# Where the products with v, the tail's score maxima, two copies and one v halving stand in a fused attention and two-MLP kernel

## The chip, the core and the metric

One core of a Trainium2 chip runs the kernel. The metric is device time in microseconds (us), the median of the runs. The engines are TensorE (PE, with its weight loads shown apart as PEld), VectorE (DVE), ScalarE (ACT), GpSimd (POOL) and SyncE (SP), whose queue issues every DMA here.

## The reference, cut to what matters

```python
# q, k, v: [4, 8, 576, 64], f: [4, 8, 576], all float32
scores = q @ k^T / 8 + (cum[:, :, :, None] - cum[:, :, None, :])   # cum = cumsum(log f); causal
attn = softmax(scores)                                             # rows of 576, masked above the diagonal
x  = (attn @ v) -> [2304, 512]                                     # heads side by side
x1 = (s * relu(x @ w_in)**2 + b) @ w_out                           # d_ff 2048
out = leaky(x1 @ w2_in, 0.01) @ w2_out                             # d_ff 2048
```

## The kernel before

Tokens are cut into nine units: for each of the 4 batches the first 256 positions ("first" units), for each batch the next 320 ("rest" units, of which the last 64 positions are the tail), and one unit that gathers the four tails' results. The first MLP works unit by unit, in 16 steps each. A step does h (12 products, L941), then g on ACT and DVE (Relu, Square, copy to the high half on ACT, the low half by a subtraction on DVE), then o (12 products, L990) with the g of two steps earlier. Each float32 operand is split in a high and a low half, hence three products for one. The first two units run together ("joint"), and the second MLP follows after the last unit.

The attention of later units is laid between the first MLP's steps. A **pair** of heads of a rest unit takes four steps; there are 16 such pairs, one after another:

- step 0: scores of 128 queries against 512 keys for both heads (tile `ps_s`); per head a score maximum on DVE (L334, it writes tile `tt`), the exponent on ACT (L356), a high half in f16 on ACT (`p_high`, L410) and a low half on DVE (`p_low`, L415), which a DMA then transposes into `p_t` (L423). Of the second head the halves are written only in the next step ("carry").
- step 1: the same with 384 keys.
- step 2: the tail, 64 queries of both heads against 576 keys, in the middle of the step, after h.
- step 3: no scores; the next pair's v is scaled and halved (L241 to L260) and transposed into `v_st`.

The products of p with v (`av_mm`, L467) come three steps after their scores: of the 512-key tiles in step 3, of the 384-key tiles in the next pair's step 0, of the tail in its step 1. `av_copy` (ACT, L493) and `av_add` (DVE, L497) then bring the two halves of the product together in `x_raw` or `x_l`.

All of that is written inside `in_order()`: on each engine instructions run exactly in the order of the code, so an engine whose next instruction waits holds back everything behind it. `ps_s` is a single buffer: new scores wait until the maxima of the former ones are taken. The pool `tt` has 4 buffers, `p_hl` 3.

At the end of the joint units `mlp1_end` reads four sums out of PSUM through `x1o` tiles (pool `tt`) in turn on ACT (L1018) and DVE (L1020), each followed by a DMA to DRAM. This stands in the first step of the third unit, while two `tt` buffers still hold exponents that wait for `diags` (DVE, L381 to L715) and the products that turn them (L725).

Of the kernel before, what the change touches and what calls it, by code (L numbers as in the profile page):

```python
# [8 lines left out]
F32 = mybir.dt.float32  # L9
# [8 lines left out]
P = 128  # L18
UN = 256
# [20 lines left out]
def attention_moe_moe_kernel(  # L40
# [274 lines left out]
    def st_score(i):  # L315
        mm_score(i)
        score_max(i)
        score_exp(i)
# [166 lines left out]
    def av_copy(i):  # L485
        jb, n, ts, last = tiles[i]
        u, h, j, half = jobs[jb]
        if last and not half and h % 2 == 0:
            x_raw[j // 2] = xp.tile([P, UN], F32, tag="x_raw", name="x_raw", bufs=1)
        if half:  # L490
            x_l[j // 2] = xp.tile([P, NL], F32, tag="x_l", name="x_l", bufs=1)
        for o, own, oth in av_parts(i):
            nc.scalar.copy(o, oth)  # L493
# [302 lines left out]
    plan = {}  # L796

    def at_step(n):
        return plan.setdefault(n, {k: [] for k in ("v", "s", "av", "x", "turn", "first", "load")})

    t_of = {}
    for i, (jb, *_) in enumerate(tiles):
# [2 lines left out]
    for p in range(H, NP):  # L805
        ids = t_of[p]
        at_step(nxt)["s"] = ids[:2]
        if len(ids) == 2:
            at_step(nxt + 1)["turn"] = at_step(nxt + 2)["first"] = ids
            nxt += 2  # L810
            if len(t_of[p + 1]) > 2:
                at_step(nxt)["load"].append(p + 1)
                at_step(nxt + 1)["v"].append((p + 1, 0))
                nxt += 2
                at_step(nxt)["v"].append((p + 1, 1))
        else:
            for k in range(3):
                at_step(nxt + k)["s"] = ids[2 * k : 2 * k + 2]
                at_step(nxt + 3 + k)["av"] += ids[2 * k : 2 * k + 2]
            at_step(nxt + 6)["x"].append(ids[-1])  # L820
            if p + 1 < NP:
                at_step(nxt + 3)["v"] += [(p + 1, 0), (p + 1, 1)]
            nxt += 4
# [17 lines left out]
    def attend(n):  # L841
        e = at_step(n)
        first = e["s"] and len(t_of[jobs[tiles[e["s"][0]][0]][2] // 2]) == 2
        tail = e["s"] and jobs[tiles[e["s"][0]][0]][3]
        if ended:
            mlp1_end(*ended.pop())
        dg.update({k: diags(k) for k in e["turn"]})
        if e["first"]:
            k = e["first"][-1]
            first_x(3, jobs[tiles[k][0]][1] // 2, pair_av(3, k))  # L850
        for i in e["av"]:
            av_mm(i)
        if e["s"] and not tail:
            mm_score(e["s"][0])
        for i in carry:
            p_high(i)
            p_low(i)
        carry.clear()
        for i in e["av"]:
            av_copy(i)  # L860
        if tail:
            assert not e["av"]
            return
        for i in e["s"]:
            score_max(i)
        for i in e["s"]:
            score_exp(i)
        if len(e["v"]) > 1:
            v_part(*e["v"].pop(0))
        for k, i in enumerate(e["s"]):  # L870
            if not first:
                p_scale(i)
            if k == 0:
                for a in e["av"]:
                    av_add(a)
        if not e["s"]:
            for a in e["av"]:
                av_add(a)
        if not first:
            for i in e["s"][:1]:  # L880
                p_high(i)
                p_low(i)
            carry.extend(e["s"][1:])

    dg = {}

    def attend_mid(n):
        e = at_step(n)
        turn_pair(e["turn"])
        for i in e["s"]:  # L890
            if jobs[tiles[i][0]][3]:
                st_score(i)
                p_scale(i)
                p_high(i)
                p_low(i)
# [51 lines left out]
                )  # L947
        return ps

    def mlp1_g(u, i, ps):  # L950

        n = UN + 2 * (u == UB)
        if joint[0]:
            r = r_all.rearrange("p u n -> p (u n)")
            g = gp.tile([P, 2, 2 * UN], F32R, tag="g", name="g", bufs=2)
            nc.scalar.activation(r, ps, AF.Relu)  # L956
            nc.scalar.activation(r, r, AF.Square)
            nc.scalar.copy(g[:, 0], r)
            rest.append(lambda: nc.vector.tensor_tensor(out=g[:, 1], in0=r, in1=g[:, 0].bitcast(F32), op=ALU.subtract))
            return g  # L960
        if u != UB:
            if i % 2 == 0:
                kept["g"] = gp.tile([P, 2, 2, UN], F32R, tag="g", name="g", bufs=2)
            g = kept["g"][:, i % 2]
        else:
            g = gp.tile([P, 2, UN + 2], F32R, tag="g", name="g", bufs=2)
        if u == UB:
            nc.gpsimd.memset(g[:, 0, UN:].bitcast(F32), 1.0)
            nc.gpsimd.memset(g[:, 1, UN:].bitcast(F32), 0.0)
        nc.scalar.activation(ps, ps, AF.Relu)  # L970
        nc.scalar.activation(ps, ps, AF.Square)
        nc.scalar.copy(g[:, 0, :UN], ps)  # L972
        nc.vector.tensor_tensor(out=g[:, 1, :UN], in0=ps, in1=g[:, 0, :UN].bitcast(F32), op=ALU.subtract)  # L973
        return g[:, :, :n]

# [22 lines left out]
    def mlp1_end(u, po):  # L998
        if 1 < u < UB:
            b, u0 = units[u][:2]  # L1000
            for k, po in enumerate(po):
                if k == 0:
                    o = wt_tile().bitcast(F32).rearrange("p (k n) -> p k n", k=2)
                    nc.scalar.mul(o, po, sb[:, 0:1])
                else:
                    o = r_all
                    nc.vector.tensor_scalar(o, po, sb[:, 0:1], None, ALU.mult)  # L1007
                last = nc.sync.dma_start(
                    out=x1d[2 * k * P : 2 * (k + 1) * P, b * S + u0 : b * S + u0 + UN].rearrange("(k p) t -> p k t", p=P),
                    in_=o,  # L1010
                )
            return last
        for d in (2, 1, 0, 3) if u < 2 else range(ND):
            x1 = x1d[d * P : (d + 1) * P, :]
            if u < 2:
                o = ap.tile([P, S], F32, tag="tt", name="x1o", bufs=4)[:, : 2 * UN]
                if d % 2 == 0:
                    nc.scalar.mul(o, po[d], sb[:, 0:1])  # L1018
                else:
                    nc.vector.tensor_scalar(o, po[d], sb[:, 0:1], None, ALU.mult)  # L1020
                last = nc.sync.dma_start(
                    out=x1.rearrange("p (b s) -> p b s", b=B)[:, :2, :UN], in_=o.rearrange("p (b s) -> p b s", b=2)
                )
                continue
            if d == 0:
                o2 = wt_tile().bitcast(F32).rearrange("p (k n) -> p k n", k=2)
            o = (r_all if d < 2 else o2)[:, d % 2]
            if u == UB:
                nc.vector.tensor_scalar(bw1[:, d : d + 1], po[d][:, UN : UN + 1], sb[:, 1:2], None, ALU.mult)
            if d % 2 == 0:  # L1030
                nc.scalar.mul(o, po[d][:, :UN], sb[:, 0:1])
            else:
                nc.vector.tensor_scalar(o, po[d][:, :UN], sb[:, 0:1], None, ALU.mult)
            if u < NU - 1:
                b, u0 = units[u][:2]
                last = nc.sync.dma_start(out=x1[:, b * S + u0 : b * S + u0 + UN], in_=o)
            else:
                last = nc.sync.dma_start(
                    out=x1.rearrange("p (b s) -> p b s", b=B)[:, :, S - NL :],
                    in_=o.rearrange("p (b s) -> p b s", b=B),  # L1040
                )
        return last
# [134 lines left out]
        pending.append((1, i, g))  # L1177
        high(w1, c_of, i)

    def first_mlp(u, i, mid=lambda: None):  # L1180
        ps = mlp1_h(u, i)
        g = mlp1_g(u, i, ps)
        mid()
        while pending and (len(pending) > 1 or pending[0][0] == 1 or u == UB):
            mlp1_back(u)
        pending.append((u, i, g))

    last = None
    for u in range(1, NU):
# [12 lines left out]
        for i in range(NF):  # L1202
# [10 lines left out]
            if u < NU - 2:  # L1213
                n = (u - 2) * NF + i
                with in_order():
                    if n == 0:
                        rest.pop()()
                        for k in range(ND):
                            first_x(2, k, x_held[k])
                    attend(n)  # L1220
                    if n == 1:
                        attend_mid(n)
                        first_mlp(u, i)
                    else:
                        first_mlp(u, i, lambda: attend_mid(n))
                    attend_end(n)
                continue
            with in_order():
# [98 lines left out]
```

## Time and profile before

| | us |
|---|---|
| median of 3 runs | 1025.35 (1024.13 to 1030.38) |
| the profiled execution, its own time | 1027.19 |
| its span, first to last instruction | 1025.3 |
| PE busy in the span | 977.6 (95%) |
| DVE busy | 526.1 (51%) |
| ACT busy | 502.2 (49%) |

The engines' shares are means over stages: the short pairs of the first units end near 205 us, the 16 long pairs run from 210 to about 511, and from there on PE has hardly any pause. A wait is put down to the instruction that released it; whether that instruction sets the pace has to be followed further back.

### The profile page before, as it was taken

To read this page: it belongs to the slowest core of one execution; us is meant where nothing else is said; L and a number is where in the kernel's file an instruction comes from. 1 tells how busy PE (TensorE), PEld (TensorE's weight loads), DVE (VectorE), ACT (ScalarE), POOL (GpSimd) and SP (SyncE) were. 2 spreads that over 40 slices of the span, in tenths; PEclk is the share of its full clock that TensorE was granted. 3 is DMA by queue.
4 is the path that set the end of the run, shared out by engine and by line. 5 is a ranking of instruction groups with operands and counts; after the bars stand their busy time and mean duration, and the time that the engine had idled before them with its cause. 6 is when DMAs were issued, how large, how long until landed. Compare 5 with 4: busy or idle time off the path is not lost.

```text
span 1025.3 us, 17139 instructions
## 1 busy us (share of the span) xinstructions
PE 977.6 (95%) x6464; PEld 835.4 (81%) x6464; DVE 526.1 (51%) x1383; ACT 502.2 (49%) x1196; POOL 27.7 (3%) x100
## 2 busy tenths in 40 slices
PE   5899998989999999999999999999999999999998
PEld 3667776878888888888899998888888888888897
DVE  5888763357677677677612379886111211211111
ACT  4777664556667666666643466543212222221232
POOL 1000000000000000000000000000000000000000
PEclk9999999999999999999999999999999999999999
DMA  8844022359989989889410497002100100100010
GB/s 289 302 131 162 21 82 66 93 112 177 199 174 182 188 169 205 182 159 195 92 43 1 148 376 258 1 1 73 52 1 1 61 1 1 42 1 1 1 42 21
DMA packets 157074, 110.32 MB, mean 108 GB/s; under 512 B 110592, under 2 KB 135168, under 8 KB 156992
## 3 DMA queue, kind: packets, MB, share of 16 engines
q1 hardware_dynamic: 156992, 109.23, 42.7%
q8 instruction: 51, 0.84, 0.3%
q14 instruction: 31, 0.25, 0.1%
HBM read 74.00 MB, written 10.04 MB: 82 GB/s over the span
## 4 chain that ended last, share of the span: by engine, by line
PE 53%; DMA 1%; DVE 0%; issue 0%; POOL 0%; ACT 0%; POOLq 0%
PE ps_o L1090 20%; PE ps_h L1074 19%; PE ps_o L990 6%; PE ps_h L941 6%; DMA p_t<-p_hl 0%; PE ps_v L467 0%; DMA p_t<-p_hl_t 0%; PE ps_s L300 0%; PE ps_s L287 0%; DVE p_hl_t L415 0%; POOL v_hl L254 0%; ACT p_hl_t L410 0%; DVE r_all L1007 0%; DVE o L1102 0%; DVE vs L241 0%
## 5 line engine op out<-in xcount | busy, mean ns | idle before, releaser
L941 PE MATMUL ps_h<-x_all,w 128*128 128x256 f32 (+1 forms) x1536 | 232.6, 300 | 1.2 <-ACT r_all L956 0.7
L990 PE MATMUL ps_o<-g,w 128*128 128x256 f32 (+2 forms) x1536 | 227.8, 297 | 2.7 <-DVE r_all L1007 2.7
L1090 PE MATMUL ps_o<-w,g 128*128 128x512 f32 x864 | 215.0, 395 | 0.0
L990 PEld LDWEIGHTS ps_o<-g,w 128*128 128x128 f32 x1536 | 203.2, 189 | 14.2 <-DVE r_all L1007 3.5
L1074 PE MATMUL ps_h<-x,w 128*128 128x512 f32 (+1 forms) x960 | 213.5, 370 | 0.0
L941 PEld LDWEIGHTS ps_h<-x_all,w 128*128 128x128 f32 x1536 | 202.7, 190 | 11.4 <-issue 1.2
L1074 PEld LDWEIGHTS ps_h<-x,w 128*128 128x128 f32 x960 | 169.1, 188 | 34.4
L1090 PEld LDWEIGHTS ps_o<-w,g 128*128 128x128 f32 x864 | 161.0, 188 | 37.5
L1082 DVE TENSOR_TENSOR g<-ps_h,g 128x512 fp32r<-128x512 f32 (+1 forms) x80 | 50.9, 637 | 248.7 <-ACT g L1081 248.4
L1080 ACT ACTIVATE ps_h<-ps_h 128x512 f32<-128x512 f32 (+1 forms) x80 | 43.1, 539 | 263.2 <-PE ps_h L1074 263.2
L356 ACT ACTIVATE tt<-tt,sm 128x512 f32<-128x512 f32 (+4 forms) x128 | 76.1, 597 | 91.6 <-DVE sm L334 91.6
L973 DVE TENSOR_TENSOR g<-ps_h,g 128x256 fp32r<-128x256 f32 x112 | 47.3, 422 | 98.3 <-ACT g L972 97.6
L970 ACT ACTIVATE ps_h<-ps_h 128x256 f32<-128x256 f32 x112 | 40.9, 366 | 52.9 <-PE ps_h L941 52.9
L334 DVE CUSTOM_DVE_ANT_0 tt<-ps_s,cumk 128x512 f32<-128x512 f32 (+4 forms) x128 | 58.8, 497 | 4.4 <-PE av L734 2.0
L467 PE MATMUL ps_v<-p_t,v_st 128*128 128x128 f16 (+1 forms) x768 | 44.3, 208 | 15.3 <-DMA p_t<-p_hl_t 8.7
L467 PEld LDWEIGHTS <-v_st 128*128 128x128 f16 x768 | 36.7, 98 | 19.6 <-issue 17.3
L415 DVE SCALAR_TENSOR_TENSOR p_hl<-tt,sm,p_hl 128x512 f16<-128x512 f32 (+1 forms) x64 | 43.9, 685 | 8.0 <-ACT p_hl L410 6.3
L1081 ACT CAST g<-ps_h 128x512 fp32r<-128x512 f32 (+1 forms) x80 | 43.5, 544 | 6.5 <-PE ps_o L1090 4.1
L300 PE MATMUL ps_s<-qk_p 64*128 64x512 f32 (+3 forms) x224 | 44.4, 492 | 1.5 <-DVE sm L334 1.3
L114 DVE SCALAR_TENSOR_TENSOR wt<-w_raw,wt 128x512 int32<-128x512 int32 x64 | 44.3, 692 | 2.0
L972 ACT CAST g<-ps_h 128x256 fp32r<-128x256 f32 x112 | 41.7, 372 | 4.3
L109 ACT ACTIVATE wt<-w_raw 128x512 f32<-128x512 f32 x64 | 41.3, 673 | 4.6 <-DMA w_raw<-in_moe_w_in 3.8
(113 smaller groups left out, 785.4 us busy)
## 6 DMA issues: line engine op xcount, KB each, us to landing
w_raw<-in_moe_w_in SPq DMA_DIRECT2D x32, 512.0 KB, 8.3
w_raw<-in_moe_w_out SPq DMA_DIRECT2D x32, 512.0 KB, 9.1
cumk<-cumd SPq DMA_DIRECT2D x32, 256.0 KB, 4.0
qk_p<-in_qk SPq DMA_DIRECT2D x16, 480.0 KB, 4.6
cumk<-cumd SPq DMA_DIRECT2D x32, 144.0 KB, 3.3
v_raw<-in_v SPq DMA_DIRECT2D x16, 288.0 KB, 3.3
out<-o SPq DMA_DIRECT2D x18, 256.0 KB, 2.1
x2r<-x1d SPq DMA_DIRECT2D x4, 1024.0 KB, 5.5
```

The costliest lines, as they stand in the source:

```text
L114: nc.vector.scalar_tensor_tensor(x, top, -0x80000000, x, ALU.bitwise_and, ALU.bitwise_or)
L300: nc.tensor.matmul(ps[:, e, at[r] : at[r + 1]], qk[rows, q0 - u0 : q0 - u0 + m], qk[rows, qn : qn + q0 + m], start=(r == 0), stop=False,)
L334: nc.vector.tensor_tensor_reduce(tt[:, at + k0 : at + k0 + kw], ps[:, c, :kw] if half else ps[:, h % 2, at : at + w], cumk[jb][:, k0 : k0 ...
L356: nc.scalar.activation(e, e, AF.Exp, bias=sm[:, r : r + 1], scale=-1.0, accum_out=sm[:, 2 + r : 3 + r])
L415: nc.vector.scalar_tensor_tensor(v[:, 1, :w], e, inv, v[:, 0, :w], ALU.mult, ALU.subtract)
L467: nc.tensor.matmul(av[:, at + e * m : at + (e + 1) * m], v_st[j + e][:, k].rearrange("p l d -> p (l d)"), pt[:, to + l * nk + k, e * m : ( ...
L941: nc.tensor.matmul(ps, wi[:, a, d * P : (d + 1) * P], x_all[:, :, c, d] if joint[0] else x[:, c, d], start=(d == 0 and n == 0), stop=(d == ...
L973: nc.vector.tensor_tensor(out=g[:, 1, :UN], in0=ps, in1=g[:, 0, :UN].bitcast(F32), op=ALU.subtract)
L990: nc.tensor.matmul(po[d], wo[:, a, d * P : (d + 1) * P], g[:, c], start=(first and n == 0), stop=(last and n == 2),)
L1074: nc.tensor.matmul(ps[:, :n], wi[:, a, d * P : (d + 1) * P], x[:, e, d, :n], start=(d == 0 and k == 0), stop=(d == ND - 1 and k == 2),)
L1082: nc.vector.tensor_tensor(out=g[:, 1, :n], in0=raw, in1=g[:, 0, :n].bitcast(F32), op=ALU.subtract)
L1090: nc.tensor.matmul(po[m], g[:, a, m * P : (m + 1) * P], wo[:, e, :], start=(i == 0 and k == 0), stop=(i == NF - 1 and k == 2),)
```

## The change

Four edits. (1) In `attend` the products with v, their copies and additions leave the head of the step; they stand in `attend_mid`, after h and after g's instructions. (2) The tail's scores, maxima and exponent are called from inside `mlp1_g`, ahead of the subtraction that makes g's low half; scaling and halving stay in `attend_mid`. (3) Two of the four `x1o` tiles come from the pool `p_hl`. (4) The halving of the first long pair's v moves from the end of its step to just behind the exponents.

```diff
-                at_step(nxt)["v"].append((p + 1, 1))
+                at_step(nxt)["early"].append((p + 1, 1))
...
-        for i in e["av"]:
-            av_mm(i)
         if e["s"] and not tail:
             mm_score(e["s"][0])
         for i in carry:
             p_high(i)
             p_low(i)
         carry.clear()
-        for i in e["av"]:
-            av_copy(i)
...
         for i in e["s"]:
             score_exp(i)
+        for p, part in e["early"]:
+            v_part(p, part)
         if len(e["v"]) > 1:
             v_part(*e["v"].pop(0))
-        for k, i in enumerate(e["s"]):
-            if not first:
+        if not first:
+            for i in e["s"]:
                 p_scale(i)
-            if k == 0:
-                for a in e["av"]:
-                    av_add(a)
...
+    def attend_tail(n):
+        for i in at_step(n)["s"]:
+            if jobs[tiles[i][0]][3]:
+                st_score(i)
+
     def attend_mid(n):
         e = at_step(n)
         turn_pair(e["turn"])
+        for part in (av_mm, av_copy, av_add):
+            for i in e["av"]:
+                part(i)
         for i in e["s"]:
             if jobs[tiles[i][0]][3]:
-                st_score(i)
                 p_scale(i)
...
         nc.scalar.copy(g[:, 0, :UN], ps)
+        early()
         nc.vector.tensor_tensor(out=g[:, 1, :UN], in0=ps, in1=g[:, 0, :UN].bitcast(F32), op=ALU.subtract)
...
-                o = ap.tile([P, S], F32, tag="tt", name="x1o", bufs=4)[:, : 2 * UN]
+                o = p_tile(F32) if d in (0, 3) else ap.tile([P, S], F32, tag="tt", name="x1o", bufs=4)[:, : 2 * UN]
...
-                        first_mlp(u, i, lambda: attend_mid(n))
+                        first_mlp(u, i, lambda: attend_tail(n), lambda: attend_mid(n))
```

On ACT, from the start of a pair's step 0 to its step 1, the order before is:

```order
L356 ACTIVATE tt,sm<-tt,sm 128x512 x2
L410 ACTIVATE p_hl<-tt,sm 128x512
L970 ACTIVATE ps_h<-ps_h 128x256
L971 ACTIVATE ps_h<-ps_h 128x256
L972 CAST g<-ps_h 128x256
L410 ACTIVATE p_hl<-tt,sm 128x512
L493 COPY x_l<-ps_v 64x64 x2
L356 ACTIVATE tt,sm<-tt,sm 128x384 x2
```

and in the change:

```order
L356 ACTIVATE tt,sm<-tt,sm 128x512 x2
L410 ACTIVATE p_hl<-tt,sm 128x512
L967 ACTIVATE ps_h<-ps_h 128x256
L968 ACTIVATE ps_h<-ps_h 128x256
L969 CAST g<-ps_h 128x256
L493 COPY x_raw<-ps_v 64x256 x2
L410 ACTIVATE p_hl<-tt,sm 128x512
L356 ACTIVATE tt,sm<-tt,sm 128x384 x2
```

The copies into `x_raw` stood ahead of the first row and now stand between g's copy and the second head's high half; those into `x_l` move in the same way to the next step.

On DVE, from the second head's low half of the 384 keys (step 2) to the tail's scaling, before:

```order
L415 SCALAR_TENSOR_TENSOR p_hl<-tt,sm,p_hl 128x384
L973 TENSOR_TENSOR g<-ps_h,g 128x256
L334 ISA tt,sm<-ps_s,cumk 128x288
L334 ISA sm 128x1
L334 ISA tt,sm<-ps_s,cumk,sm 128x288
L334 ISA sm 128x1
L392 TENSOR_SCALAR sm<-sm 128x1
```

and in the change:

```order
L415 SCALAR_TENSOR_TENSOR p_hl<-tt,sm,p_hl 128x384
L334 ISA tt,sm<-ps_s,cumk 128x288
L334 ISA sm 128x1
L334 ISA tt,sm<-ps_s,cumk,sm 128x288
L334 ISA sm 128x1
L971 TENSOR_TENSOR g<-ps_h,g 128x256
L392 TENSOR_SCALAR sm<-sm 128x1
```

The subtraction of g has moved behind the tail's maxima. On PE step 0 was products with v, scores, h, o and is now scores, h, products with v, o; step 1 changes in the same way, and step 3 from products with v, h, o to h, products with v, o.

## Rows read from the trace of the kernel before

**Rows 1.** Stretches: window, length, busy PE PEld DVE ACT POOL, clock, DMA share, GB/s.

```profile
170.00:175.00 5.00, 4.71 (x26) 4.61 (x28) 1.06 (x6) 0.95 (x3) 0.00 (x0) 0.66 0.23 79
225.00:230.00 5.00, 4.04 (x44) 3.94 (x43) 2.99 (x9) 2.22 (x6) 0.99 (x2) 1.00 1.08 274
250.00:300.00 50.00, 47.36 (x442) 41.88 (x441) 36.59 (x115) 33.24 (x87) 2.93 (x7) 1.00 0.92 178
```

**Rows 2.** Waits, whole run: who waited for whom, us in total, times, longest.

```profile
PE ps_v L467 <- DMA p_t<-p_hl_t: 8.7, 9, 1.8
...
PE ps_t L725 <- DVE diag L715: 6.8, 5, 4.6
...
PE ps_v L467 <- DMA p_t<-p_hl: 6.4, 11, 2.7
...
ACT p_hl L410 <- DMA p_t<-p_hl: 2.3, 3, 1.1
```

**Rows 3.** Timeline of PE: start, us, engine, line, operation, tiles, count, [idle before].

```profile
285.11 1.13 PE L300 MATMUL ps_s<-qk_p 64*128 64x512 f32 x4
...
302.27 1.13 PE L300 MATMUL ps_s<-qk_p 64*128 64x512 f32 x4
```

**Rows 4.** Timeline of ACT and DVE through one pair of long heads.

```profile
288.32 0.68 DVE L334 CUSTOM_DVE_ANT_0 tt<-ps_s,cumk 128x512 f32<-128x512 f32 x1
...
291.88 0.37 ACT L972 CAST g<-ps_h 128x256 fp32r<-128x256 f32 x1
...
292.15 0.73 ACT L410 ACTIVATE p_hl<-tt,sm 128x512 f16<-128x512 f32 x1
...
292.90 0.43 ACT L493 COPY x_l<-ps_v 64x64 f32<-64x64 f32 x2
292.91 0.75 DVE L415 SCALAR_TENSOR_TENSOR p_hl<-tt,sm,p_hl 128x512 f16<-128x512 f32 x1 [0.20 <-ACT p_hl L410]
293.57 0.55 DVE L334 CUSTOM_DVE_ANT_0 tt<-ps_s,cumk 128x384 f32<-128x384 f32 x1
...
297.60 0.62 DVE L415 SCALAR_TENSOR_TENSOR p_hl<-tt,sm,p_hl 128x384 f16<-128x384 f32 x1
...
298.68 0.42 DVE L973 TENSOR_TENSOR g<-ps_h,g 128x256 fp32r<-128x256 f32 x1 [0.46 <-ACT g L972]
299.02 0.45 DVE L334 CUSTOM_DVE_ANT_0 tt<-ps_s,cumk 128x288 f32<-128x288 f32 x1
...
300.98 0.15 DVE L392 TENSOR_SCALAR sm<-sm 128x1 f32<-128x1 f32 x1 [0.94 <-ACT tt L356]
...
303.29 0.37 ACT L972 CAST g<-ps_h 128x256 fp32r<-128x256 f32 x1
...
303.68 0.74 ACT L493 COPY x_raw<-ps_v 64x256 f32<-64x256 f32 x2
...
306.55 0.68 DVE L334 CUSTOM_DVE_ANT_0 tt<-ps_s,cumk 128x512 f32<-128x512 f32 x1
...
325.44 0.68 DVE L334 CUSTOM_DVE_ANT_0 tt<-ps_s,cumk 128x512 f32<-128x512 f32 x1
```

**Rows 5.** Timeline around the joint units copies, PE and DVE.

```profile
168.79 0.75 DVE L1020 TENSOR_SCALAR x1o<-ps_o,sb 128x512 f32<-128x512 f32 x1 [2.77 <-DMA x1d<-x1o]
...
170.28 2.74 PE L725 MATMUL ps_t<-diag,tt 128*128 128x128 f32 x12 [4.56 <-DVE diag L715]
...
172.68 2.20 PE L941 MATMUL ps_h<-x_all,w 128*128 128x256 f32 x12
...
176.67 1.67 PE L941 MATMUL ps_h<-x_all,w 128*128 128x256 f32 x12
...
181.51 1.70 PE L725 MATMUL ps_t<-diag,tt 128*128 128x128 f32 x12 [0.32 <-DVE diag L715]
```

**Rows 6.** Timeline of PE and DVE in the first long pair.

```profile
225.96 0.61 PE L467 MATMUL ps_v<-p_t,v_st 128*128 128x128 f16 x8 [2.71 <-DMA p_t<-p_hl]
...
231.44 0.69 DVE L334 CUSTOM_DVE_ANT_0 tt<-ps_s,cumk 128x512 f32<-128x512 f32 x1 [0.87 <-PE ps_s L311]
```

More of the change, by code (lines that the diff above doesn't have):

```diff
@@ L798, in at_step @@
     def at_step(n):
-        return plan.setdefault(n, {k: [] for k in ("v", "s", "av", "x", "turn", "first", "load")})
+        return plan.setdefault(n, {k: [] for k in ("v", "early", "s", "av", "x", "turn", "first", "load")})
     t_of = {}
@@ L858, in attend @@
         carry.clear()
-        for i in e["av"]:
-            av_copy(i)
         if tail:
-            assert not e["av"]
             return
@@ L867, in attend @@
             score_exp(i)
+        for p, part in e["early"]:
+            v_part(p, part)
         if len(e["v"]) > 1:
             v_part(*e["v"].pop(0))
-        for k, i in enumerate(e["s"]):
-            if not first:
+        if not first:
+            for i in e["s"]:
                 p_scale(i)
-            if k == 0:
-                for a in e["av"]:
-                    av_add(a)
[L876 to L879, printed above, removed]
             for i in e["s"][:1]:
@@ L948, in mlp1_h, with mlp1_g @@
         return ps
-    def mlp1_g(u, i, ps):
+    def mlp1_g(u, i, ps, early=lambda: None):
         n = UN + 2 * (u == UB)
@@ L1178, in joint_step, with first_mlp @@
         high(w1, c_of, i)
-    def first_mlp(u, i, mid=lambda: None):
+    def first_mlp(u, i, early=lambda: None, mid=lambda: None):
         ps = mlp1_h(u, i)
-        g = mlp1_g(u, i, ps)
+        g = mlp1_g(u, i, ps, early)
         mid()
```

## The prediction

> **What bounds the kernel now.** I read the table of stretches first. While the long pairs run, PE is busy 47.36 of 50 us, DVE 36.59, ACT 33.24 [rows 1]: PE looks like the bound, with little to win. Then the list of waits: PE's pauses there are named after transposed probabilities, 8.7 us for the tail's and 6.4 us for the others, and once in the joint units 4.6 us after `diag` [rows 2]. The question is whether these pauses are the cause of the pace or its mark. Two timelines answer it. On PE, one pair of four steps that holds no pause lasts 302.27 - 285.11 = 17.16 us [rows 3]. On DVE, the first score maximum of a pair follows that of the pair before after 306.55 - 288.32 = 18.23 us, and after 325.44 - 306.55 = 18.89 us where a unit's result is read out in between [rows 4]. In that stretch no maximum waits for PE: 293.57, 299.02 and 306.55 all start straight behind other DVE work. So ACT and DVE, each free a quarter to a third of the time but passing every tile to and fro, make a chain of 18.23 us a pair; PE could do 17.16 and waits for the rest, some 1.1 us a pair. A change is worth what it takes off this chain, until PE's 17.16 is met. In the one PE-bound place ahead of it, the end of the joint units, PE stands 4.56 us [rows 5].
>
> **The change part by part**, against the profiled execution's own time, 1027.19 us (its span 1025.3 and 1.9 around it).
>
> *Joint units' copies.* DVE's second copy waited 2.77 us for the DMA that empties an `x1o` buffer, and `diag`, PE's releaser, is queued behind it [rows 5]. With two tiles from `p_hl`, whose last readers (the copies into `x_all` at the head of this step) are done, that wait goes: 2.8 us off PE's pause, 1.8 us of it left, for the copies themselves and the scaling behind them. Behind the pause the granted clock was 0.66 over 170 to 175 [rows 1], and the 12 turning products took 2.74 against 1.70 us, the 12 of h 2.20 against 1.67 [rows 5]: 1.57 us more. Whether a pause of 1.8 us costs clock no row of this place shows; the nearest is the pause of 2.71 us that ended at 225.96 [rows 6], and the stretch behind it has clock 1.00 [rows 1]. I take the whole: -4.3 us; between -2.8 (clock still falls) and that. ACT's copies are freed too, but nobody waits for them. From there to 210 us PE sets the pace, so this arrives whole.
>
> *Products with v behind h.* PE does the same products; each wait for `p_t` gets the cover of an h (1.67 us [rows 5]) and, for two of three, of the scores. By that the 15.1 us of such waits would go. But PE's order is not the chain. On it, the copies and additions have moved. Before, ACT copied `x_raw` behind g's copy of step 3 (303.29, 303.68, 0.74 us), where it then waited for the next maxima: free of charge. Now the pair stands between g's copy of step 0 and the second head's high half. That half began 292.15 - 291.88 = 0.27 us behind g's copy [rows 4]. Now the copy begins 0.39 us behind it (303.68 - 303.29) and takes 0.74, so the half begins 1.13 us behind: +0.86. The low half on DVE follows the high half by 0.76 us (292.91 - 292.15), and the maxima of the 384 keys follow it at once (293.57): all of it is on the chain. In step 1 the `x_l` copies, 0.43 us, do the same: 0.39 + 0.43 - 0.27 = +0.55. I let nothing overlap behind a copy, since every copy here starts where its forerunner ends (292.15 + 0.73 = 292.88 against 292.90). The additions on DVE are no longer than g's subtraction, 0.42 us for as many columns and twice the partitions [rows 4], so 0.84 for the two of step 0; between that subtraction (0.40 + 0.34 behind ACT's copy of g: 291.88 to about 292.62) and the low half (1.13 + 0.76 behind it) lie 1.15 us in which DVE only waits: nothing. In step 1 they have a quarter of the columns and 0.7 us. Without that cover they would add up to 1.3 us a pair.
>
> *Tail's maxima ahead of g's low half.* DVE's last low half of the 384 keys starts at 297.60, the tail's maximum at 299.02, 1.42 us later, with g's subtraction and a wait of 0.46 for ACT between [rows 4]. Put directly behind, it starts 0.53 us after (a half of 0.75 us is followed after 0.66, 293.57 - 292.91, so one of 0.62 after 0.53): -0.89. The subtraction of 0.42 us falls into the 0.94 us in which DVE waits for the tail's exponent [rows 4]: free. g is used two steps later, and its `ps_h` bank one step and more later.
>
> Together a pair changes by 0.86 + 0.55 - 0.89 = **+0.52 us**: the chain becomes 18.75 us. The first pair has no copies before it; over the 14 that follow: +7.3 us. Below: all copies covered after all, -0.89 a pair, -12.5. Above: nothing saved at the tail, +1.41 a pair, +19.7. I take the middle because each of its three terms is a distance between two rows.
>
> *First pair.* It gains the 0.89 at its tail, and at its end DVE no longer waits 0.87 us for scores that PE gave late, behind its own 2.71 us pause for `p_t` [rows 6]: -1.8. The earlier halving of v does the same work; SP issues v's transposes ahead of those of p, which PE needs only in step 3: nothing, or either way one such instruction: 0.75 us for 512 columns [rows 4], so an estimated 0.9 for its 640.
>
> *Waits for a `p_hl` buffer.* Three times ACT waited for a transposition to free one, 2.3 us in all, 1.1 at most [rows 2]. The instruction concerned is the second high half of the 384 keys, now 1.41 us later while the buffer is filled as early as before: -2.3, between 0 and that.
>
> *End.* The last pair's tail needs no pause on PE any more (8.7/9 = 1.0 us for one): -0.5, between 0 and -1.0.
>
> The sum: -4.3 + 7.3 - 1.8 - 2.3 - 0.5 = **-1.6 us**: 1025.6 for such an execution. The median of the runs shown, 1025.35, lies 1.8 lower than the profiled one; on it the forecast is **1023.8 us**, no change that a measurement of this kernel can tell (about 1%, 10 us).
>
> One rule speaks for much more. The Trainium skill, Perfetto Trace Analysis, Optimization Strategy (under Identifying Performance Opportunities): find the gaps on the engine you optimise, see which semaphore it waits on, and make that dependency start sooner or complete faster; the section before it picks that engine by its occupancy. By it PE's waits for `p_t` are what to remove, which is the first rival. The trace disagrees with picking by occupancy: at 73% DVE is in the chain that sets 18.23 us.
>
> **The rivals.**
>
> - *The pauses are the cause* (0.14). With the waits for `p_t` covered, the pairs run at PE's 17.16: 14 x -1.07 = -15.0 in place of +7.3, so 1023.8 - 22.3 = **1002**. For it: the waits' names, and that PE's work without a pause is that short. Against it: no maximum waits for PE, so PE's speed is not what DVE lacks.
> - *Slower: PE's tail scores come too late for the maxima* (0.06). If PE, now held at the scores of 384 keys until the maxima of 512 are done, delivers the tail's scores after DVE's last low half, DVE stands in front of them, g's subtraction is queued behind, and the 0.89 is lost while the copies cost their 1.41: +19.7 in place of +7.3, **1036**. PE starts some 1.4 us into the pair, behind two maxima of 0.68, and has to do two scores (1.13 at most [rows 3]), two h and an o (1.67 at most [rows 5]) and the tail's products (under 1) before: 9.7 us in. DVE gets there at 297.60 + 0.53 - 288.32 + 1.41 = 11.2. So it decides from 1.5 us more on PE, and I give it little.
> - *The two `p_hl` tiles are not free in time* (0.06): the copies still wait, the 4.3 us stay, **1028**.
>
> The forecast keeps 0.74. Its own range is 1016 to 1031: a pair's term within about 0.5 us of +0.52, the joint units' and the buffers' terms at either bound. The range of 1013 to 1030 leaves out the first two rivals. Faster by over 1% (under 1015): the first rival and a rest of the forecast, 0.17. Slower by over 1% (above 1035.6): 0.05. Same: 0.78.
>
> **What the profile after would show.** PE's waits for `p_t` down to 2 us or less; in their place a wait of the 384-key scores (L300) on DVE's `sm` (L334) of 1 to 2 us in nearly every pair, about 20 us in all; first maxima of successive pairs 18.7 to 18.8 us apart, 19.4 at a unit's end; ACT's second high half 1.1 us behind g's copy; the tail's maximum 0.5 us behind the last low half; PE's pause before the turning products 1.8 us, with clock 1.00 behind it. Maxima under 18.2 us apart would make me wrong towards faster, DVE waiting for PE's scores towards slower.

## The result, and the profile after

The change runs in **1032.33 us** (1030.64 to 1033.49, nine runs) against 1026.12 (1021.37 to 1030.38) for the kernel before: ratio 1.0061, 95% interval 1.0041 to 1.0081. The forecast of 1023.8 with 1013 to 1030 missed it, by sign and by range. The profiled execution's span is 1030.3 us, 5.0 above the 1025.3 of before.

First the list of PE's waits after: engine, line and tile, released by; us in total, times, longest.

```profile
PE ps_s L300 <- DVE sm L334: 14.2, 14, 1.6
...
PE ps_t L725 <- DVE diag L715: 3.4, 5, 1.7
```

The waits for `p_t` of [rows 2], 15.1 us, are gone to the last one. In their place PE's 384-key scores wait in 14 of the 16 pairs for DVE's 512-key maxima, 14.2 us where the forecast had about 20. The stretches after (window, length, busy PE, PEld, DVE, ACT, POOL, clock, DMA share, GB/s):

```profile
165.00:170.00 5.00, 3.66 (x32) 3.36 (x32) 2.04 (x9) 1.51 (x5) 0.00 (x0) 1.00 0.62 211
300.00:350.00 50.00, 45.43 (x413) 39.13 (x410) 35.62 (x107) 32.22 (x82) 3.71 (x8) 1.00 0.90 173
```

PE is busy 45.43 of 50 us among the long pairs, where it was 47.36 [rows 1]: fewer named waits for data, and less work done in the time. The timeline of ACT and DVE shows the pace and one whole pair, as in [rows 4] (start, us, engine, line, operation, tiles, count, idle before):

```profile
206.83 0.69 DVE L334 CUSTOM_DVE_ANT_0 tt<-ps_s,cumk 128x512 f32<-128x512 f32 x1
...
224.26 0.68 DVE L334 CUSTOM_DVE_ANT_0 tt<-ps_s,cumk 128x512 f32<-128x512 f32 x1
...
282.56 0.68 DVE L334 CUSTOM_DVE_ANT_0 tt<-ps_s,cumk 128x512 f32<-128x512 f32 x1
...
286.12 0.37 ACT L969 CAST g<-ps_h 128x256 fp32r<-128x256 f32 x1
286.52 0.74 ACT L493 COPY x_raw<-ps_v 64x256 f32<-64x256 f32 x2
286.52 0.42 DVE L971 TENSOR_TENSOR g<-ps_h,g 128x256 fp32r<-128x256 f32 x1 [0.32 <-ACT g L969]
287.29 0.72 ACT L410 ACTIVATE p_hl<-tt,sm 128x512 f16<-128x512 f32 x1
287.30 0.86 DVE L497 TENSOR_TENSOR x_raw<-ps_v,x_raw 64x256 f32<-64x256 f32 x2 [0.35 <-ACT x_raw L493]
288.19 0.75 DVE L415 SCALAR_TENSOR_TENSOR p_hl<-tt,sm,p_hl 128x512 f16<-128x512 f32 x1
288.97 0.56 DVE L334 CUSTOM_DVE_ANT_0 tt<-ps_s,cumk 128x384 f32<-128x384 f32 x1
...
292.08 0.37 ACT L969 CAST g<-ps_h 128x256 fp32r<-128x256 f32 x1
292.48 0.42 ACT L493 COPY x_l<-ps_v 64x64 f32<-64x64 f32 x2
...
292.93 0.62 ACT L410 ACTIVATE p_hl<-tt,sm 128x384 f16<-128x384 f32 x1
292.93 0.46 DVE L497 TENSOR_TENSOR x_l<-ps_v,x_l 64x64 f32<-64x64 f32 x2
...
293.58 0.69 DVE L415 SCALAR_TENSOR_TENSOR p_hl<-tt,sm,p_hl 128x384 f16<-128x384 f32 x1 [0.18 <-ACT p_hl L410]
...
294.30 0.46 DVE L334 CUSTOM_DVE_ANT_0 tt<-ps_s,cumk 128x288 f32<-128x288 f32 x1
...
301.85 0.68 DVE L334 CUSTOM_DVE_ANT_0 tt<-ps_s,cumk 128x512 f32<-128x512 f32 x1
```

The pair lasts 301.85 - 282.56 = 19.29 us; it was 18.23 [rows 4]. Cut in three at the first maxima of the 384 keys and of the tail:

| leg of the pair, us | before | after | difference | forecast |
|---|---|---|---|---|
| 512-key to 384-key maximum | 5.25 | 6.41 | +1.16 | +0.86 |
| 384-key to tail maximum | 5.45 | 5.33 | -0.12 | -0.34 |
| tail maximum to next pair | 7.53 | 7.55 | +0.02 | 0 |
| sum | 18.23 | 19.29 | +1.06 | +0.52 |

The third leg, the same before and after, is not one of ACT and DVE alone: the next pair's first maximum stands behind the low half of v (DVE, L260), which waits 0.75 us for GpSimd's v (L254) in both kernels.

On PE the joint units' pause, in the rows that answer to [rows 5], and the queue of the first pair:

```profile
166.34 1.70 PE L725 MATMUL ps_t<-diag,tt 128*128 128x128 f32 x12 [1.70 <-DVE diag L715]
...
167.80 1.67 PE L938 MATMUL ps_h<-x_all,w 128*128 128x256 f32 x12
...
208.97 2.65 SPq L265 DMA_TRANSPOSE v_st<-v_hl  x2
211.72 0.52 SPq L214 DMA_DIRECT2D v_raw<-in_v  x1
212.35 2.67 SPq L423 DMA_TRANSPOSE p_t<-p_hl  x2
```

The pause is 1.70 us instead of 4.56, and the products behind it run at clock 1.00 (165 to 170) in 1.70 and 1.67 us instead of 2.74 and 2.20.

The spans' difference closes from these numbers: the joint units' pause began 1.1 us earlier (164.64 against 165.72; over all twelve kernels it begins between 162.8 and 166.0 us, with edit 3 or without, so no edit is credited with it); the joint copies gave 4.3; the first pair gave 19.23 - 17.43 = 1.8; the rest of the long stretch, from the second pair's first maximum to the sixteenth's, took 496.82 - 224.26 = 272.56 us against 491.76 - 231.44 = 260.32, +12.2. So -1.1 - 4.3 - 1.8 + 12.2 = +5.0.

### The profile page after: what moved, and what is told of

It is laid out like the page before. It is cut to its first block, busy times and chain, and to the rows that moved or that the text cites. A ratio compares the mean times of both kernels' runs of the same rounds, so it can differ in the third digit from the quotient of the medians.

```text
span 1030.3 us, 17155 instructions
## 1 busy us (share of the span) xinstructions
PE 984.2 (96%) x6464; PEld 836.7 (81%) x6464; DVE 532.4 (52%) x1383; ACT 505.0 (49%) x1196; POOL 27.5 (3%) x100
## 4 chain that ended last, share of the span: by engine, by line
PE 50%; ACT 0%; DVE 0%; issue 0%
PE ps_o L1088 20%; PE ps_h L1072 19%; PE ps_o L988 6%; PE ps_h L938 5%; PE ps_v L467 0%; DVE o L1100 0%; ACT tt L356 0%; ACT p_hl L410 0%; DVE g L971 0%; ACT g L969 0%; ACT ps_h L968 0%; ACT ps_h L967 0%
## 5 line engine op out<-in xcount | busy, mean ns | idle before, releaser
L988 PE MATMUL ps_o<-g,w 128*128 128x256 f32 (+2 forms) x1536 | 232.1, 300 | 5.4 <-DVE r_all L1005 5.4
L967 ACT ACTIVATE ps_h<-ps_h 128x256 f32<-128x256 f32 x112 | 40.9, 365 | 51.8 <-PE ps_h L938 51.8
L300 PE MATMUL ps_s<-qk_p 64*128 64x512 f32 (+3 forms) x224 | 44.9, 495 | 16.4 <-DVE sm L334 14.2
L968 ACT ACTIVATE ps_h<-ps_h 128x256 f32<-128x256 f32 x112 | 41.3, 369 | 3.5
```

The costliest lines, as they stand in the source:

```text
L300: nc.tensor.matmul(ps[:, e, at[r] : at[r + 1]], qk[rows, q0 - u0 : q0 - u0 + m], qk[rows, qn : qn + q0 + m], start=(r == 0), stop=False,)
L988: nc.tensor.matmul(po[d], wo[:, a, d * P : (d + 1) * P], g[:, c], start=(first and n == 0), stop=(last and n == 2),)
```

## The experiments

Theory: the copies and additions that edit 1 put on ACT's and DVE's way lengthen their chain, and cost more than all the rest saves. Rival: the loss lies in PE's new order itself, or in the tail. The pace below is between first 512-key maxima of pairs without a unit's end in between; a time is compared with before in the same set of runs (1026.1 for the change and e1 to e4, 1025.8 for e5 to e8, 1026.5 for e9 and e10).

| kernel | what runs | pace | time, us | ratio to before, interval |
|---|---|---|---|---|
| change | edits 1 to 4 | 19.28 | 1032.33 | 1.0061, 1.0041 to 1.0081 |
| e1 | 2, 3, 4 | 17.36 | 1009.07 | 0.9836, 0.9812 to 0.9861 |
| e2 | 1 | 19.97 | 1047.87 | 1.0212, 1.0187 to 1.0237 |
| e3 | 3 | 18.23 | 1022.63 | 0.9964, 0.9950 to 0.9979 |
| e4 | 2 | 17.36, some 18.2 | 1018.75 | 0.9921, 0.9891 to 0.9950 |
| e5 | change, copies and additions in idle places | 17.36 | 1006.34 | 0.9806, 0.9791 to 0.9822 |
| e6 | change, lower partitions last | 18.83 | 1025.25 | 0.9997, 0.9983 to 1.0011 |
| e7 | change, additions alone in idle places | 18.82 | 1025.19 | 0.9994, 0.9979 to 1.0009 |
| e8 | 1, 2, 3 | as change | 1031.99 | 1.0054, 1.0040 to 1.0068 |
| e9 | 4 | 18.23 | 1024.86 | 0.9991, 0.9968 to 1.0013 |
| e10 | e5, lower partitions last | 17.49 | 1007.21 | 0.9820, 0.9778 to 0.9863 |

**One edit undone, one edit alone (e1, e2).** In e1 the products with v, their copies and additions go back to the head of the step; in e2 they alone move.

```diff
# e1, against the change (e2 is the reverse, against the kernel before)
+        for i in e["av"]:
+            av_mm(i)
         if e["s"] and not tail:
             mm_score(e["s"][0])
...
-        for part in (av_mm, av_copy, av_add):
-            for i in e["av"]:
-                part(i)
...
```

> The changed kernel with its first edit undone: the products with v, their copies and additions stand at the head of the step again; the tail's maxima, the copies through p_hl and the earlier halving stay. Theory (the ACT-DVE chain sets the pace of the long pairs): the copies and additions lie in ACT's and DVE's idle time again, the tail's 0.89 us a pair is kept, so first maxima come 18.23 - 0.89 = 17.3 us apart (PE's own work is 17.16), waits for p_t come back without harm, and the time is 1026 - 4.3 - 12.5 - 1 = about 1008 us. Rival (PE's pauses for p_t set the pace, and the products at the head make them): those pauses come back at 15 us, maxima stay 18.2 us apart, and only the joint units' 4.3 us are won: about 1021 us.

> The kernel before with the first edit alone (products with v, copies and additions behind h). Theory: the x_raw copies and additions cost 1.16 us a pair as in the changed kernel's trace (2.85 us from g's copy to the maxima of 384 keys against 1.69), the x_l ones some 0.6 with g's subtraction still ahead of the tail's maxima; the chain becomes about 20.0 us, 14 pairs make +24, the first pair and the buffer waits give back 3: about 1047 us, with p_t waits on PE near zero. Rival (p_t pauses set the pace): without them 1011 us or less.

Measured 1009.07 and 1047.87: both as the theory had it. Edit 1 costs 1032.3 - 1009.1 = 23 us in the change and 22 us alone. Rows of e1, PE's waits for `p_t`, and then a stretch of e1 and one of e2:

```profile
PE ps_v L467 <- DMA p_t<-p_hl_t: 4.3, 5, 1.4
...
PE ps_v L467 <- DMA p_t<-p_hl: 2.6, 5, 1.4
```

```profile
250.00:300.00 50.00, 49.15 (x463) 43.32 (x463) 37.71 (x118) 36.05 (x94) 3.94 (x9) 1.00 0.98 189
```

```profile
250.00:300.00 50.00, 43.41 (x397) 37.41 (x395) 34.98 (x103) 30.22 (x77) 3.57 (x8) 1.00 0.82 165
```

e1 keeps 6.9 us of the very waits that edit 1 is rid of, and is 23 us faster: those pauses are not the cause of the pace. e2, without one long `p_t` wait, leaves PE 6.6 us of 50 idle.

**The other two parts alone (e3, e4).**

```diff
# e3, against the kernel before
-                o = ap.tile([P, S], F32, tag="tt", name="x1o", bufs=4)[:, : 2 * UN]
+                o = p_tile(F32) if d in (0, 3) else ap.tile([P, S], F32, tag="tt", name="x1o", bufs=4)[:, : 2 * UN]
# e4, against the kernel before
         nc.scalar.copy(g[:, 0, :UN], ps)
+        early()
...
-                st_score(i)
...
```

> The kernel before with the third edit alone (two of the joint units' copies through p_hl). Theory: PE's pause before the turning products falls from 4.56 to 1.7 us and the clock does not fall behind it: -4.3 us, 1021.8, with the long pairs at 18.23 us as before. Rival (the clock's fall has another cause): -2.8 us, 1023.3. Rival (the 4.3 us are taken back later): no change.

> The kernel before with the second edit alone (tail's maxima ahead of g's low half). Theory: 0.89 us less a pair on the chain, 17.34 us between first maxima, PE's pauses for p_t shrink by themselves because the pace comes near PE's own 17.16: -12.5 over 14 pairs, -0.9 in the first: about 1013 us. Rival (p_t pauses set the pace; the tail's p_t comes 0.9 us earlier and nothing else): nine waits of 1 us each at the tail go, -8: 1018 us, other p_t waits stay at 6 us. Rival (a second wait takes its place): no change.

e3 came within 0.8 us of its number. The first rival's 1023.3 lies inside the interval too (about 1021.0 to 1023.9), so the time does not decide between them; the trace does: the joint pause is 1.69 us, as in the change, and the clock behind it 1.00 (165 to 170). The profiled execution gives part of the gain back in the first long pair, 22.48 us against 19.23. PE there, and the stretch behind it:

```profile
221.30 1.01 PE L467 MATMUL ps_v<-p_t,v_st 128*128 128x128 f16 x8 [3.38 <-DMA p_t<-p_hl]
```

```profile
221.00:226.00 5.00, 4.70 (x26) 4.70 (x26) 1.95 (x5) 1.18 (x4) 0.99 (x2) 0.50 1.03 258
```

Here PE's wait of 3.38 us for `p_t` is followed by 5 us at the lower clock.

e4 reached 1018.75, nearer to its rival's 1018 than to the theory's 1013; its eight runs spread from 1012.87 to 1025.37, so the median does not decide, but the pace does. The pairs that nothing disturbs run at 17.36, the forecast's -0.89 taken from 18.23, where the rival leaves the pace as it was. Others stay at 18.1 to 18.2, and one took 21.38: there PE waited 2.56 us for the tail's `p_t` (at 412.83), and the clock was 0.72 and 0.60 in the stretches 410 to 415 and 415 to 420. With the chain so short, PE's waits for `p_t` do begin to count, and e4 has no cover for them. Why they fall in these pairs and not in those of e1 was not settled.

**Copies and additions moved to where ACT and DVE only wait (e5).** PE's order stays that of the change. The `x_raw` copies come right behind the second head's high half instead of ahead of it, in the trace some 0.6 us later, and ahead of the next exponents; their additions come behind the first scaling. The `x_l` copies go ahead of the tail's exponent, their additions behind g's subtraction.

```diff
# against the change
+        late_copy(n)
...
+            for k, i in enumerate(e["s"]):
                 p_scale(i)
+                if k == 0:
+                    late_add(n)
...
-        for part in (av_mm, av_copy, av_add):
-            for i in e["av"]:
-                part(i)
+        for i in e["av"]:
+            av_mm(i)
...
```

> The changed kernel with the products with v left behind h on PE, but their copies and additions put into idle time: the x_raw copies behind the second high half of 512 keys of the next step, its additions behind the first scaling there; the x_l copies ahead of the tail's exponent, its additions behind g's subtraction in that step. Theory: the chain is 17.3 to 17.4 us a pair as without the first edit, with PE's waits for p_t covered as well, so 1 to 3 us better than the run without the first edit (1009.1): about 1007 us. Rival (the products' place on PE itself costs, by later results or a later release of PSUM): near the changed kernel's 1032. Rival (the new places lie on the chain as well): 0.4 us or more a pair, 1013 us or above.

1006.34 us, as expected, and 19.5 below before: the fastest kernel of all. A stretch of e5:

```profile
250.00:300.00 50.00, 49.95 (x470) 43.92 (x469) 38.19 (x117) 34.99 (x91) 3.94 (x9) 1.00 0.93 190
```

PE is busy 49.95 of 50 us, so whether the chain or PE itself sets the 17.36 here is not told apart. PE's new order does no harm: it is the same in the change, and all that lies between the change and e5, 1032.3 - 1006.3 = 26.0 us, comes from where ACT and DVE do the copies and additions.

**Which of the two, and how (e6, e7).** e7 moves only the additions, e6 leaves all in place and lets copies and additions write partitions 64 to 127 first and 0 to 63 last.

```diff
# e7, against e5: the copies back behind the products
-        late_copy(n)
...
-        for i in e["av"]:
-            av_mm(i)
+        for part in (av_mm, av_copy):
+            for i in e["av"]:
+                part(i)
# e6, against the change
-        for e in () if not last else range(2) if half else [h % 2]:
+        for e in () if not last else (1, 0) if half else [h % 2]:
...
+        ids = e["av"] if len(e["av"]) < 2 or tiles[e["av"][0]][1] == 0 else e["av"][::-1]
```

> The changed kernel with each pair of copies and additions in the other order: partitions 64 to 127 first, 0 to 63 last. No work is added or left out. Theory (the unforeseen 0.1 to 0.2 us behind the additions come from an instruction on partition 0 that does not overlap one that began on partition 64; by the Trainium skill, VectorE: DVE Perf Modes, Two Vector instructions with no wait between them, such a one is held until all before it have finished): low half behind the additions and the maxima behind it start 0.2 us earlier in step 0, 0.1 to 0.2 in step 1, so maxima 18.9 to 19.0 us apart in place of 19.28, about 1028 us. Rival (the order of the halves makes no difference): 19.28 and 1032 us.

> The changed kernel with the copies where they are and only the additions moved to the idle places (behind the first scaling of step 1, behind g's subtraction of step 2). Theory: the copies on ACT cost what was forecast, 0.90 and 0.58 us a pair, and the additions on DVE the unforeseen rest of 0.5; so 18.75 to 18.85 us a pair and 14 x 0.45 = 6 us less than the changed kernel: about 1026 us. Rival (the rest lies with the copies): 19.28 us and 1032. Rival (the additions are the whole cost): below 18 us a pair, 1013.

e7 lands at 18.82 us a pair, where the forecast's 18.75 had been. Rows of e7:

```profile
283.76 0.37 ACT L983 CAST g<-ps_h 128x256 fp32r<-128x256 f32 x1
...
284.92 0.72 ACT L410 ACTIVATE p_hl<-tt,sm 128x512 f16<-128x512 f32 x1
285.68 0.75 DVE L415 SCALAR_TENSOR_TENSOR p_hl<-tt,sm,p_hl 128x512 f16<-128x512 f32 x1 [1.09 <-ACT p_hl L410]
286.35 0.55 DVE L334 CUSTOM_DVE_ANT_0 tt<-ps_s,cumk 128x384 f32<-128x384 f32 x1
...
290.95 0.62 DVE L415 SCALAR_TENSOR_TENSOR p_hl<-tt,sm,p_hl 128x384 f16<-128x384 f32 x1 [0.66 <-ACT p_hl L410]
...
291.49 0.45 DVE L334 CUSTOM_DVE_ANT_0 tt<-ps_s,cumk 128x288 f32<-128x288 f32 x1
```

The low half stands 0.76 behind the high half and the maximum 0.67 behind the low half; in the change these are 0.90 and 0.78. In step 1 the tail's maximum comes 0.54 behind its low half, in the change 0.72; 0.08 of these 0.18 is the low half itself, which takes 0.69 us there instead of 0.62, and what lengthens it was not followed. Rows of e6:

```profile
283.74 0.37 ACT L972 CAST g<-ps_h 128x256 fp32r<-128x256 f32 x1
284.14 0.74 ACT L493 COPY x_raw<-ps_v 64x256 f32<-64x256 f32 x2
...
284.79 0.72 ACT L410 ACTIVATE p_hl<-tt,sm 128x512 f16<-128x512 f32 x1
284.92 0.86 DVE L497 TENSOR_TENSOR x_raw<-ps_v,x_raw 64x256 f32<-64x256 f32 x2 [0.34 <-ACT x_raw L493]
285.70 0.73 DVE L415 SCALAR_TENSOR_TENSOR p_hl<-tt,sm,p_hl 128x512 f16<-128x512 f32 x1
286.36 0.54 DVE L334 CUSTOM_DVE_ANT_0 tt<-ps_s,cumk 128x384 f32<-128x384 f32 x1
```

With the lower partitions last the high half starts at 284.79, before the copies end at 284.88; in the change it starts 0.03 behind their end. The low half likewise starts 0.08 before the additions' end (285.78), the maximum 0.07 before the low half's (286.43). So an order of two equal instructions is worth 0.45 us a pair and 7 us of the kernel. This is not the same 0.45 as in e7: e7 takes the additions away and keeps the late high half on ACT, e6 keeps the additions. e6 beat its expectation of 1028, which had left ACT out: in step 1 the second high half begins 0.73 us behind g's copy instead of 0.85, and the low half follows it.

On DVE this is what the Trainium skill, VectorE: DVE Perf Modes, "Two Vector instructions with no wait between them", calls held: an instruction whose input or output begins in another group of 32 partitions than the last one read from or written to that memory starts only when all before it have finished. The trace agrees: the low half writes SBUF at partition 0 behind an addition that wrote it at 64, and begins 0.03 us behind that addition's end; the maximum reads PSUM at partition 0 while the last reader of PSUM, the second addition, began at 64, and it begins 0.03 us behind the low half's end instead of 0.08 ahead of it. That ACT does the same (0.12 us a time) is shown by the rows here alone.

**The first pair (e8, e9).** e8 is the change with the halving of v back at the step's end; e9 is the kernel before with that edit alone.

```diff
# e8, against the change (e9 has the reverse, against the kernel before)
-                at_step(nxt)["early"].append((p + 1, 1))
+                at_step(nxt)["v"].append((p + 1, 1))
```

> The changed kernel with its fourth edit undone: the first long pair's v is halved at the end of its step again. Theory now (the transposes of v then stand between the two of p on SP's queue and the second p_t comes 3 us later; the h ahead of the products covers 1.7 us of that): a pause of about 1 us on PE in the first pair that the chain does not notice or only by some tenths, so 0 to 1 us, 1032 to 1033. Rival (the fourth edit is what removed the first pair's pause): the first pair back at 19.2 us, 1034. As forecast before the result: nothing.

> The kernel before with edit 4 alone (the first v halved, its transpose between the two of h). Theory, from the first pair of the change with edit 4 undone (19.49 us, against 17.43 with it): edit 4 alone takes the first pair from 19.23 to 17.4 to 18.4 us between first score maxima, PE's wait for the transposed h there goes, every other pair stays at 18.23 and the unit's end at 18.9; the time is 1 to 2 us lower, 1024 to 1025 us. Rival, the forecast's: the first pair's gain came from the joint's end and edit 4 does nothing, first pair 19.2 and time as before.

Neither time can be told from its counterpart, but the traces can. In e8 the first pair took 19.49 us instead of 17.43, as its rival had it. PE, SP's queue and DVE in e8:

```profile
210.16 2.67 SPq L265 DMA_TRANSPOSE v_st<-v_hl  x2
212.93 0.53 SPq L214 DMA_DIRECT2D v_raw<-in_v  x1
213.58 1.24 SPq L423 DMA_TRANSPOSE p_t<-p_hl  x1
...
219.57 0.61 PE L467 MATMUL ps_v<-p_t,v_st 128*128 128x128 f16 x8 [2.16 <-DMA p_t<-p_hl]
...
224.43 0.69 DVE L334 CUSTOM_DVE_ANT_0 tt<-ps_s,cumk 128x512 f32<-128x512 f32 x1 [1.99 <-PE ps_s L311]
```

Halved late, v's transposes and the load of `v_raw` stand in SP's queue between the two transposes of p: the second was issued 213.58 + 1.24 - 204.94 = 9.9 us behind the pair's first maximum, in the change 212.35 + 2.67 - 206.83 = 8.2 us behind it. PE waits 2.16 us for it, the clock behind that pause is 0.70 (219 to 224), and DVE waits 1.99 for PE. So with edits 1 to 3 the first pair's gain needs edit 4. The queue's order alone does not make the pause, though. e2, edit 1 without edit 4, has the order of e8, and PE does not wait there: its first pair took 231.98 - 213.69 = 18.29 us, close to the undisturbed pace before, 18.23. The second transposition of p landed 3.6 us behind its issue in e2, 5.9 in e8 and 5.1 in the kernel before; what makes it slow was not followed. And e9 shows that edit 4 alone doesn't bring the gain: its first pair took 230.24 - 211.09 = 19.15 us, which is the rival's number and not the theory's 17.4 to 18.4. PE in e9:

```profile
221.51 1.07 PE L467 MATMUL ps_v<-p_t,v_st 128*128 128x128 f16 x16
...
227.05 0.49 PE L467 MATMUL ps_v<-p_t,v_st 128*128 128x128 f16 x6 [1.56 <-DMA p_t<-p_hl]
227.77 0.49 PE L467 MATMUL ps_v<-p_t,v_st 128*128 128x128 f16 x6 [0.23 <-DMA p_t<-p_hl]
```

The wait at the 512-key products (2.71 us in [rows 6]) is gone, and 1.56 + 0.23 us of it come back at the 384-key products, one step later, ahead of the next pair's scores on PE. Only with edit 1, which puts scores and an h before those products, does this wait go too: e1, with edits 2 to 4, keeps it (1.43 us), and e2 and e8, with edit 1, have none.

**A control (e10).** e5's places with e6's order.

```diff
# against e5
-        for e in () if not last else range(2) if half else [h % 2]:
+        for e in () if not last else (1, 0) if half else [h % 2]:
...
+        return ids if len(ids) < 2 or tiles[ids[0]][1] == 0 else ids[::-1]
...
```

> The change with its copies and additions in idle places, as before, and with partitions 64 to 127 first and 0 to 63 last in them. Theory: the hold on the next instruction costs only where that instruction is on the chain; in the idle places nothing on the chain follows, so the pace stays at 17.35 to 17.36 us and the time within 1 us of 1006.3. Rival: the hold shortens the chain anyhow, 0.2 us a pair and more, so about 1003 us.

1007.21 us, no gain, as the theory has it. But the pace is 17.49, 0.13 above what was expected, and the rows show where that arises: on ACT, behind the first high half of 384 keys. First e5, then e10:

```profile
283.73 0.60 ACT L410 ACTIVATE p_hl<-tt,sm 128x384 f16<-128x384 f32 x1
284.23 0.36 ACT L987 ACTIVATE ps_h<-ps_h 128x256 f32<-128x256 f32 x1
```

```profile
284.95 0.60 ACT L410 ACTIVATE p_hl<-tt,sm 128x384 f16<-128x384 f32 x1
285.58 0.37 ACT L991 ACTIVATE ps_h<-ps_h 128x256 f32<-128x256 f32 x1
```

In e5 g's Relu starts 0.10 us before the high half ends, in e10 0.03 behind its end, and so in 15 of the 16 pairs; the rest of the pair keeps that delay. A copy into one half of the partitions reads PSUM in the other half. With the swapped order the last copy has read PSUM from partition 64 on, and Relu, the next reader of PSUM on ACT, begins at 0. So on ACT the swap frees the next writer and holds the next reader of PSUM, and that one is on the chain. e6 pays the same 0.12 us there and gains more elsewhere. The theory that nothing on the chain follows the copies was wrong by this much.

## Why the prediction was wrong

- **What bounds the kernel: right.** The pace is set by the chain of ACT and DVE. The first rival, that the pauses for `p_t` are the cause (1002 us), fell: the change removes all of them and the pairs became slower, and e1 keeps 6.9 us of them at 17.36 a pair. That the fastest kernel, e5, comes within 5 us of that rival's time is no proof of it; e5 took the copies off the chain.
- **Joint copies, -4.3: right**, in size and in place; a pause of 1.70 us was followed by clock 1.00, and so in all eight kernels with edit 3. The reason given for it, a pause of 2.71 us elsewhere that cost no clock, was weak: other pauses below 2.71 us did cost clock (last section).
- **Copies, +0.86 and +0.55 a pair: right.** e7 to e5, the copies alone, is 18.82 - 17.36 = 1.46 us against 1.41. The second high half began 287.29 - 286.12 = 1.17 us behind g's copy, forecast 1.13.
- **The step that failed: the additions, "nothing".** They cost 0.45 us a pair (19.28 - 18.82, e7), 7.1 us in all. The working set their 0.84 us beside a gap of 1.15 us in which DVE only waits. It didn't ask when their input comes: the first addition started only when both copies were done, 287.30, and both ended at 288.16, so the low half came 0.14 us late. And it let the instructions behind them follow at the distances seen before, where no half-height instruction stood ahead: 0.12 us more to the 384-key maximum, 0.18 to 0.19 to the tail's, 0.08 of it in a longer low half. This is why the tail's -0.89, right by itself (e4, 17.36), came out smaller in the change.
- The rest of the pair's error, 0.07 us, is what stays in e7 (18.82 against 18.75). With +1.05 in place of +0.52, 14 pairs give +14.7 instead of +7.3; that alone turns -1.6 into +5.8. The term's error of 0.53 us lies just beyond the "about 0.5 us" allowed for it, and the stated upper end of 1030 lies below even the working's own 1031.
- **First pair, -1.8: the number is right, its reason only in part.** The tail's 0.89 is there, and edit 1 alone does take PE's pause away in e2 (18.29 us). But "the earlier halving of v does the same work ... nothing" was wrong: with edit 4 undone the pair is back at 19.49 (e8). The forecast looked at when PE needs p's transposes and not at what stands between them in SP's queue, nor at how long they take to land. How much of the 1.8 is edit 4's stays open.
- **`p_hl` waits, -2.3: right.** ACT's waits for a transposition to free a buffer are gone, and 14 x 1.05 = 14.7 exceeds the +12.2 measured by 2.5. **End, -0.5:** nearly nothing; what the other terms leave of the spans' +5.0 is under 0.1 us.
- **Slower by late tail scores (1036): fell.** The tail's maximum stands straight behind its low half and waits for nothing. **`p_hl` tiles not free (1028): fell**, PE's pause shows it. The kernel got slower than before by a mechanism that none of the rivals had, the additions.

## What to carry to other kernels

Where two half-idle engines pass tiles to and fro, an instruction put between one's hand-over and the next cost its full length here, and a gap on the other engine covers an addition only if its input is there when the gap begins: write the input's arrival next to the gap. The copies and additions had put 1.46 + 0.45 = 1.9 us on each pair's chain; moved by half a microsecond to two, to where both engines wait for something else, they turned a change of +6 us into one of -19. Before a pause is blamed, look whether the kernel without it is faster; and when a transfer is late, read what stands ahead of it in its queue.

## What the runs showed of the hardware

Of two instructions on the halves of the partitions, the one that comes last sets what the next may overlap, on DVE and on ACT alike. When it is on the upper half and the next begins at partition 0, the next starts 0.02 to 0.03 us behind its forerunner's end instead of 0.08 to 0.10 ahead of it: 0.1 us or a little more each time. Swapping the two gave 0.45 us a pair, 7 us of the kernel (e6). On ACT both the partition last written (e6) and the one last read from PSUM (e10) counted.

The length of a pause alone does not tell what PE's clock does behind it. At the joint units the clock fell in the four kernels with a pause of 4.56 or 4.57 us (before, e2, e4, e9) and stayed at 1.00 in the eight with 1.69 or 1.70. In the first long pair it stayed at 1.00 behind 2.71 us [rows 1, 6] and was 0.50 for 5 us behind 3.38 (e3). But it also stayed behind 2.92 us, ended at 226.03 (e4, first row), and fell, to 0.50 in part of the stretch, behind 2.16 us, ended at 219.57 (e8, second row), and behind 1.56 and 0.23 us, ended at 227.77 (e9, third row). What else decides was not found.

```profile
226.00:231.00 5.00, 4.97 (x48) 4.28 (x47) 2.77 (x7) 1.84 (x5) 0.99 (x2) 1.00 0.98 243
219.00:224.00 5.00, 4.43 (x25) 2.70 (x24) 2.64 (x7) 0.49 (x2) 0.99 (x2) 0.70 0.88 151
227.00:232.00 5.00, 4.72 (x27) 3.19 (x27) 3.33 (x11) 1.76 (x5) 0.99 (x2) 0.66 1.03 252
```
